# Retention followed by a Mish feed-forward layer: the opening rearranged (warm-up, copy of q, pools of the last y and the first h, state 4)

## The chip, the cores and the metric

The kernel runs on one core of one Trainium2 chip. The metric is device time in microseconds of one execution, the median of several runs. The engines are TensorE (PE in the profile; its weight loads are PEld), VectorE (DVE), ScalarE (ACT), GpSimd (POOL) and SyncE (SP), which here only issues transfers.

## The reference

Inputs are q, k and v of shape (4, 8, 768, 64) (batch, heads, tokens, head size) and two weight matrices. Per batch and head a 64x64 state is carried from token to token, and its output goes through a feed-forward layer:

```
gamma[h] = 1 - 2**(-5-h);  scale = 1/sqrt(64)
for t in range(768):
    state = gamma * state + outer(k[t], v[t])
    y[t]  = scale * q[t] @ state
x = y, heads side by side          # 3072 x 512
h = x @ w_in                       # 3072 x 2048
g = h * tanh(softplus(h))          # Mish
out = g @ w_out                    # 3072 x 512, float32
```

## The kernel before, in words

The tokens are taken in 24 chunks of 128. Within a chunk the recurrence is written with matmuls: scores of q and k, a triangular mask, "present" (masked scores times v), "past" (q times the state before the chunk), and the state's update ("outer" product of k and v, added to the old state, times gamma**128, the tile gcm). Powers of gamma are put into q and v when they are cast to fp16. Two heads share the 128 partitions, so a chunk has 4 pairs of heads (HP = 4).

Chunks are grouped in blocks: the first has 4 chunks (512 tokens), each of the ten others 2. For a block the finished y is copied from PSUM into an fp16 tile xt, from there `g1` makes h in units of 512 PSUM columns, `mish` on ScalarE turns each unit into g, and `g2_mm` with `g2_out` makes the output rows. From block 3 on the second product uses seven products in place of eight (`seven`); nothing there is changed. Attention work of the next block is put between the matmuls of the current one by hand-written plans (step number: functions). The order of all instructions on each engine is the order in the program (`manual_schedule`), and waits come from the tiles that they share.

Two PSUM pools matter: `mmps` (tag mm, 4 buffers of one bank) and `atps` (tag at, 2 buffers of two banks).

The first block (`first_block`, L642) is the opening, and it is built differently. Its q comes in two transfers of four heads each, with four successive tokens on each partition (`load_first_q`, L181). VectorE multiplies and casts it (L193), TensorE transposes it in 8 transposes for each half (L199), and `first_q_out` (L202) copies the result from PSUM into qfirst_t, putting the tokens back in their natural order as it writes. Half 0 of that copy is on ScalarE (L207), half 1 on VectorE (L209). k and v come with two successive tokens on a partition. ScalarE casts k (`cast_two`, L224) and copies its transposes (`turned_two`, L243); GpSimd casts v (L227). `scores_half` (L248) makes the scores of half the heads for two chunks, and `mask_half` (L261) masks them on VectorE with tri_first. `outer_first`, `state_first` (here the old state is added by an identity matmul on TensorE, L283, and VectorE multiplies by gcm, L285), `present_first` and `past_first` make y for two chunks in one tile y_ps of the at pool. `xt_out` (L304) copies y into xt: chunks 0 and 1 in one ScalarE copy, chunk 2 on ScalarE, chunk 3 on VectorE. The first two units of h are made half by half (`first_g1`, L635), in two tiles of the mm pool.

TensorE is kept busy before and between these steps by matmuls whose results are thrown away: `spin` (L339, fp16 with the identity) and `spin_wide` (L346, fp32 with the triangular mask tri). The constants ident, tri and tri_first are built by GpSimd in this order (L84 to L97). The weights w_in are loaded in slices, and each slice is cast to fp16 in halves: the first half by GpSimd, all others by VectorE (`cast_win`, L158).

Chunk 4, the first of block 1, is worked on near the end of block 0: `outer_state` (L424) makes its outer product and calls `state` (L387), where VectorE adds the old state (L394) and multiplies by gcm (L395).

Of the kernel before, what the change touches and what calls it, by code (L numbers as in the profile page):

```python
# [16 lines left out]
def kernel(  # L17
# [9 lines left out]
    nc = tc.nc  # L27
# [9 lines left out]
    R = 2  # L37
    HB = P // R
    BLOCKS = [4] + [2] * ((NCK - 4) // 2)
    first = [sum(BLOCKS[:i]) for i in range(len(BLOCKS))]  # L40
# [41 lines left out]
    gcm = cpool.tile([P, HP, P], FP32, name="gcm")  # L82
    warm = cpool.tile([P, 1], FP32, name="warm")
    nc.gpsimd.memset(ident, 0.0)  # L84
    nc.gpsimd.affine_select(
# [6 lines left out]

    tri_first = cpool.tile([P, R, C], FP32, name="tri_first")
    nc.gpsimd.memset(tri_first, 0.0)
    for c in range(2):
        t = tri_first[c * HB:(c + 1) * HB]
        nc.gpsimd.affine_select(  # L97
            out=t, in_=t, compare_op=ALU.is_gt, fill=1.0, base=0,
            pattern=[[1, R], [-1, C]], channel_multiplier=R)
    nc.vector.memset(warm, 0.0)  # L100
# [8 lines left out]

    qfirst_t = cpool.tile([P, HP, TB], FP16, name="qfirst_t")  # L110
    raw, k16s, v16s, t16s, kts, amf = {}, {}, {}, {}, {}, {}
# [89 lines left out]

    def first_q_out(half, t_ps, eng):  # L202
        n = HP // 2
        dst = qfirst_t[:, half * n:(half + 1) * n].rearrange("p i (t r) -> p i t r", r=CPB)
        src = t_ps.rearrange("p i r t -> p i t r")
        if eng is nc.scalar:
            nc.scalar.copy(dst, src)  # L207
        else:
            eng.tensor_copy(dst, src)  # L209

# [37 lines left out]
    def scores_half(s, half, at):  # L248
        for j in range(HP // 2):
            i = half * (HP // 2) + j  # L250
            for r in range(R):
                for c in range(2):
                    g = 2 * s + c
                    for hh in range(2):
                        o = slice(64 * hh, 64 * hh + 64)
                        nc.tensor.matmul(
                            at[toks(c), hh, j, r], kts[s][o, i, r, toks(c)],
                            qfirst_t[o, i, g * C:(g + 1) * C], start=True, stop=True,
                            skip_group_check=True)

    def mask_half(s, half, at):  # L261
        am = amf[s, half] = tpp.tile([P, 2, HP // 2, R, C], FP16, name="am")
        nc.vector.tensor_tensor(  # L263
            am.rearrange("p a j r t -> p (a j) (r t)"),
            at.rearrange("p a j r t -> p (a j) (r t)"),
            tri_first.rearrange("p r t -> p (r t)").unsqueeze(1).broadcast_to(
                (P, HP, R * C)), op=ALU.mult)
# [19 lines left out]
    def present_first(s, y, pairs):  # L287
        for i in pairs:
            half, j = divmod(i, HP // 2)
            for r in range(R):  # L290
                for c in range(2):
                    for hh in range(2):
                        nc.tensor.matmul(
                            y[64 * hh:64 * hh + 64, c, i], v16s[s, half][toks(c), r, 2 * j + hh],
                            amf[s, half][toks(c), hh, j, r], start=i == 0 and r == 0,
                            stop=s == 0 and c == 0 and r == R - 1, skip_group_check=True)

    def past_first(g, y):
        for i in range(HP):
            nc.tensor.matmul(  # L300
                y[:, g % 2, i], states[g - 1][:, i], qfirst_t[:, i, g * C:(g + 1) * C],
                start=False, stop=True, skip_group_check=True)

    def xt_out(g, y, eng, n=1):  # L304
        if eng is nc.scalar:
            nc.scalar.copy(xts[0][:, g:g + n], y[:, g % 2:g % 2 + n])
        else:
            eng.tensor_copy(xts[0][:, g:g + n], y[:, g % 2:g % 2 + n])

# [29 lines left out]
    def spin(at, n):  # L339
        for i in range(0, n, HP):  # L340
# [3 lines left out]
                ident.unsqueeze(1).broadcast_to((P, m, P)), start=True, stop=True)  # L344

    def spin_wide(at, n):  # L346
        nc.tensor.matmul(  # L347
            at[:, 0].rearrange("p j r t -> p (j r) t")[:, :n], tri,
            tri.unsqueeze(1).broadcast_to((P, n, C)), start=True, stop=True)

# [73 lines left out]
    def outer_state(g):  # L424
        outer(g, atps.tile([P, 2, HP, P], FP32, name="u_ps", tag="at")[:, 0])
        state(g)

# [19 lines left out]
    def y_two(blk):  # L447
# [6 lines left out]
        for j in range(2):  # L454
            present(a + j, lambda i: y_ps[:, i, j], lambda i: False)
        xts[blk] = xtp.tile([P, HP, TB], FP16, name="xt")
        nc.scalar.copy(  # L457
            xts[blk][:, :, :2 * C], y_ps.rearrange("p i j c -> p i (j c)"))

# [5 lines left out]
    def g1(blk, u):  # L465
# [3 lines left out]
        for j in range(per):  # L469
            s, f = divmod(u * per + j, FPS)  # L470
            for bp in range(NBP):
                nc.tensor.matmul(  # L472
                    h_ps[:, j], win(s, f, bp), xt(blk, bp),
                    start=(bp == 0), stop=(bp == NBP - 1))
        mish(blk, u, h_ps)

    def xt(blk, bp):
        return xts[0][:, :, bp] if blk == 0 else xts[blk][:, bp, :BLOCKS[blk] * C]

# [18 lines left out]
    def g2_out(o_ps, blk, t, due, cols=slice(None)):  # L498
        osb = op.tile(list(o_ps.shape), FP32, name="osb", tag="osb")
        nc.vector.tensor_copy(osb, o_ps)  # L500
        row0 = (first[blk] + t) * P
        dst = out[row0:row0 + P, cols]
        stores.append((due, dst, osb))
# [130 lines left out]

    def first_g1(h_ps, u, s):  # L635
        t = slice(s * TB // 2, (s + 1) * TB // 2)
        for bp in range(NBP):
            nc.tensor.matmul(  # L638
                h_ps[:, 0, t], win(0, u, bp), xts[0][:, 2 * s:2 * s + 2, bp],
                start=bp == 0, stop=bp == NBP - 1, skip_group_check=True)  # L640

    def first_block():  # L642
# [6 lines left out]
        load_weights()  # L649
        xts[0] = xtp.tile([P, CPB, HP, C], FP16, name="xt")  # L650

        at = at_tile()
        spin_wide(at, HP)
        spin_wide(at, HP)
        spin(at, 8)
        tq = turn_first_q(qf, 0)
        spin_wide(at, 3)
        first_q_out(0, tq, nc.scalar)
        tq = [tq, turn_first_q(qf, 1)]
        cast_two("k", 0, 0)  # L660
        turn_two(0, 0)
        first_q_out(1, tq[1], nc.vector)
        turned_two(0, 0)
        cast_two("k", 0, 1)
        spin_wide(at, 3)
        scores_half(0, 0, at)
# [5 lines left out]
        at = at_tile()  # L672
        spin_wide(at, 3)
        scores_half(0, 1, at)
# [9 lines left out]
        mask_half(1, 0, at)  # L684
        y = atps.tile([P, 2, HP, C], FP32, name="y_ps", tag="at")
        present_first(0, y, range(HP))
        turn_two(1, 1)
        turned_two(1, 1)
        state_first(1)
        past_first(1, y)  # L690
        xt_out(0, y, nc.scalar, 2)
        for half in range(2):
# [4 lines left out]
        mask_half(1, 1, at)  # L697
        y = atps.tile([P, 2, HP, C], FP32, name="y_ps", tag="at")
        outer_first(1)
        state_first(2)  # L700
        present_first(1, y, range(HP // 2))
        h_ps = [mmps.tile([P, 1, TB], FP32, name="h_ps", tag="mm") for _ in range(2)]
        first_g1(h_ps[0], 0, 0)
        present_first(1, y, range(HP // 2, HP))
# [3 lines left out]
        xt_out(3, y, nc.vector)  # L708
        first_g1(h_ps[1], 1, 0)
        cast_win(0, 1, nc.vector)  # L710
        for u in range(2):
            first_g1(h_ps[u], u, 1)
            mish(0, u, h_ps[u])
        state_first(3)
# [114 lines left out]
```

## Time and profile before

| | |
|---|---|
| median of 3 runs | 207.05 us (206.41 to 207.69) |
| the profiled execution's own time | 207.59 us |
| its span, first to last instruction | 205.80 us |
| busy share of the span | PE 96%, PEld 73%, DVE 58%, ACT 43%, POOL 39% |
| chain that ended last | PE 89%, DVE 5%, ACT 3% |
| mean granted TensorE clock | 0.999 |
| DMA | 38.60 MB, mean 188 GB/s |

Times within the profile are counted from the start of the span. The chain is followed back from the last instruction: at each step to what released it, or to the instruction before it on its engine. "issue" is time in which an engine waited for nothing that the profile shows. The busy time of a matmul reaches to its modelled end, and the next one starts before it; so the spacing of two starts tells what a matmul adds to a row of them, and its duration (0.2 us more or less longer) tells when its result is there. Transfers are told by issue and landing; the landings are in the trace.

### The profile page before, as it was taken

The numbers are of one execution on the slowest core, as the hardware profiler recorded it, in microseconds if no ns is written. First come the engines' busy times: TensorE is split into PE (matmuls) and PEld (weight loads), VectorE is DVE, ScalarE is ACT, GpSimd is POOL, SyncE is SP. The second block draws the span as 40 slices with busy tenths as digits, with TensorE's granted clock in tenths as the row PEclk, the third lists the DMA queues.
The fourth block names the chain that finished last, engine by engine and source line by source line (L and its number), as shares of the span: only waits on it lengthen the run. The fifth ranks groups of instructions, "written<-read, shape, count | busy, mean of one in ns | idle before, by whom it ended". The sixth has DMA issues, their size and how long they took to land.

```text
span 205.8 us, 4678 instructions
## 1 busy us (share of the span) xinstructions
PE 198.3 (96%) x1975; PEld 150.9 (73%) x1975; DVE 120.4 (58%) x179; ACT 87.7 (43%) x147; POOL 79.5 (39%) x74
## 2 busy tenths in 40 slices
PE   6988999999999999999999999999999999999993
PEld 2556444456855865888888888888888888898882
DVE  3686644168027987775686773575684773573062
ACT  2462763242621631453453453453453453552640
POOL 4261000519954757647477066077077000000000
PEclk9999999999999999999999999999999999999999
DMA  5999999998999999999795892996794800200202
GB/s 183 298 317 361 387 387 276 293 214 177 208 258 259 210 197 242 221 211 227 168 253 92 201 256 56 205 206 105 188 242 83 204 3 3 102 2 27 78 25 76
DMA packets 95892, 38.60 MB, mean 188 GB/s; under 512 B 82304, under 2 KB 89984, under 8 KB 95872
## 3 DMA queue, kind: packets, MB, share of 16 engines
q1 hardware_dynamic: 92608, 37.50, 77.8%
q10 hardware_dynamic: 3264, 0.82, 2.3%
q8 instruction: 15, 0.25, 0.5%
q14 instruction: 5, 0.04, 0.1%
HBM read 27.30 MB, written 6.29 MB: 163 GB/s over the span
## 4 chain that ended last, share of the span: by engine, by line
PE 89%; DVE 5%; ACT 3%; issue 1%; POOL 0%; POOLq 0%
PE h_ps L472 40%; PE o_ps L571 22%; PE o_ps L494 11%; PE at L368 3%; PE y_ps L411 2%; PE at L347 2%; PE y_ps L401 2%; PE u_ps L382 2%; DVE am L374 1%; DVE gsum L541 1%; ACT xt L457 1%; PE h_ps L638 1%; ACT g L488 1%; DVE am L263 1%; ACT qk L224 1%
## 5 line engine op out<-in xcount | busy, mean ns | idle before, releaser
L472 PE MATMUL h_ps<-xt,win 128*128 128x256 f16 (+1 forms) x696 | 86.1, 281 | 0.3
L488 ACT ACTIVATE g<-h_ps 128x512 f16<-128x512 f32 x96 | 57.2, 597 | 57.4 <-PE h_ps L472 56.0
L472 PEld LDWEIGHTS <-win 128*128 128x128 f16 x696 | 67.3, 98 | 15.4 <-issue 0.8
L316 POOL TENSOR_TENSOR qk<-qf,qvs 128x512 f16<-128x512 f32 x20 | 21.7, 1086 | 61.0 <-DMA qf<-in_q_dram 55.7
L374 DVE TENSOR_TENSOR am<-at,tri 128x1024 f16<-128x1024 f32 x20 | 23.6, 1219 | 15.8 <-PE at L368 15.6
L494 PE MATMUL o_ps<-wout,g 128*128 128x512 f16 x128 | 30.1, 380 | 0.0
L321 POOL TENSOR_SCALAR qk<-kf 128x512 f16<-128x512 f32 x18 | 28.6, 1587 | 3.7 <-DMA kf<-in_k_dram 2.7
L571 PEld LDWEIGHTS <-gsum 128*128 128x128 f16 x256 | 24.2, 98 | 4.4 <-DVE gsum L541 1.0
L322 POOL TENSOR_TENSOR v<-vf,qvs 128x512 f16<-128x512 f32 x20 | 21.9, 1094 | 6.3 <-DMA vf<-in_v_dram 4.9
L571 PE MATMUL o_ps<-tmat,gsum 128*128 128x256 f16 x192 | 23.9, 273 | 0.3
L494 PEld LDWEIGHTS <-g 128*128 128x128 f16 x128 | 11.7, 98 | 13.0 <-issue 0.3
L585 DVE TENSOR_TENSOR osb<-o_ps,snap 128x256 f32<-128x256 f32 x24 | 10.1, 421 | 18.3 <-ACT snap L577 15.1
L571 PEld LDWEIGHTS <-g 128*128 128x128 f16 x192 | 18.8, 98 | 2.2
L457 ACT CAST xt<-y_ps 128x1024 f16<-128x1024 f32 x10 | 10.1, 1012 | 22.8 <-PE y_ps L411 15.5
L540 DVE TENSOR_TENSOR gsum<-g 128x512 f16<-128x512 f16 x16 | 7.3, 454 | 14.2 <-ACT g L488 14.2
L571 PE MATMUL o_ps<-wout,g 128*128 128x256 f16 x128 | 15.3, 273 | 0.0
L577 ACT COPY snap<-o_ps 128x256 f32<-128x256 f32 x24 | 8.9, 372 | 14.4 <-PE o_ps L571 13.0
L394 DVE TENSOR_TENSOR su<-u_ps,st 128x512 f32<-128x512 f32 x13 | 9.0, 691 | 4.5 <-PE u_ps L382 4.3
L395 DVE TENSOR_TENSOR st<-su,gcm 128x512 f16<-128x512 f32 x13 | 10.8, 832 | 0.4
L541 DVE TENSOR_TENSOR gsum<-gsum,g 128x512 f16<-128x512 f16 x16 | 8.8, 551 | 0.5
L347 PE MATMUL at<-tri 128*128 128x384 f32 (+1 forms) x10 | 6.6, 767 | 1.9 <-POOL tri L89 1.9
L571 PE MATMUL o_ps<-tmat,g 128*128 128x256 f16 x64 | 8.3, 272 | 0.0
(72 smaller groups left out, 150.2 us busy)
## 6 DMA issues: line engine op xcount, KB each, us to landing
kf<-in_k_dram SPq DMA_DIRECT2D x23, 256.0 KB, 4.7
vf<-in_v_dram SPq DMA_DIRECT2D x23, 256.0 KB, 4.9
out_dram<-osb SPq DMA_DIRECT2D x22, 256.0 KB, 3.4
qf<-in_q_dram SPq DMA_DIRECT2D x19, 256.0 KB, 4.0
wt<-in_moe_w_out_dram SPq DMA_DIRECT2D x3, 1024.0 KB, 8.9
wi<-in_moe_w_in_dram SPq DMA_DIRECT2D x4, 512.0 KB, 7.6
wi<-in_moe_w_in_dram SPq DMA_DIRECT2D x2, 1024.0 KB, 11.9
qfirst<-in_q_dram SPq DMA_DIRECT2D x2, 512.0 KB, 4.6
```

Source lines behind the costliest of these rows:

```text
L316: nc.gpsimd.tensor_tensor(q16, qf, qs.unsqueeze(2).broadcast_to((P, H, D)), op=ALU.mult)
L321: nc.gpsimd.tensor_scalar(k16, kf, BOOST, None, op0=ALU.mult)
L322: nc.gpsimd.tensor_tensor(v16, vf, vs.unsqueeze(2).broadcast_to((P, H, D)), op=ALU.mult)
L347: nc.tensor.matmul(at[:, 0].rearrange("p j r t -> p (j r) t")[:, :n], tri, tri.unsqueeze(1).broadcast_to((P, n, C)), start=True, stop=True)
L374: nc.vector.tensor_tensor(am, ats.pop(g), tri.unsqueeze(1).unsqueeze(1).broadcast_to((P, 2, HP, C)), op=ALU.mult)
L395: nc.vector.tensor_tensor(st, su, gcm, op=ALU.mult)
L457: nc.scalar.copy(xts[blk][:, :, :2 * C], y_ps.rearrange("p i j c -> p i (j c)"))
L472: nc.tensor.matmul(h_ps[:, j], win(s, f, bp), xt(blk, bp), start=(bp == 0), stop=(bp == NBP - 1))
L488: nc.scalar.activation(gt, h_ps, AF.Mish, scale=inv_boost3)
L494: nc.tensor.matmul(o_ps, gts[blk, fb][:, t * P:(t + 1) * P], wouts[s][:, f, cols], start=(fb == 0), stop=(fb == NFB - 1))
L541: nc.vector.tensor_tensor(s2, s1, a11, op=ALU.subtract)
L571: nc.tensor.matmul(o_ps, x(f), w(f), start=first and f == 0, stop=f == n - 1, skip_group_check=True)
```

## The change

- **Constants.** GpSimd builds tri_first first, then ident, then tri. tri_first has a new order of its columns.
- **Warm-up.** `spin_wide` is gone. `spin(at, 36)` issues nine 128x512 fp16 matmuls with ident before the first q transposes, and `spin(at, 4)` one more at three later places, twelve in all.
- **q.** `first_q_out` copies without reordering, both halves on VectorE. qfirst_t keeps the tokens in the order of the transposes: token 4t+r stands at column (r, t). Scores and past read 4 pieces of 32 columns; y comes out in that order too.
- **xt of block 0** becomes one row of 512 columns for each pair of heads, in the order (r, t). `xt_out` writes 32 columns at a time; chunks 0 and 1 are two ScalarE copies instead of one. The first block's output rows are stored with a stride of four rows.
- **Pools.** y of chunks 2 and 3 is two tiles of the mm pool, and the first two units of h are one tile of the at pool (they were the other way round). Unit 0 of h is made in two halves, unit 1 in one piece after it; the half of unit 1 that was made before the last y was copied is gone.
- **State 4.** `outer_state` adds the old state with an identity matmul on TensorE, as the opening does; VectorE only multiplies by gcm.

```diff
+    Q0 = C // CPB
+    tri_first = cpool.tile([P, R, CPB, Q0], FP32, name="tri_first")
+    nc.gpsimd.memset(tri_first, 0.0)
+    for c in range(2):
+        t = tri_first[c * HB:(c + 1) * HB]
+        nc.gpsimd.affine_select(
+            out=t, in_=t, compare_op=ALU.is_gt, fill=1.0, base=0,
+            pattern=[[1, R], [-1, CPB], [-CPB, Q0]], channel_multiplier=R)
     nc.gpsimd.memset(ident, 0.0)
...
-    tri_first = cpool.tile([P, R, C], FP32, name="tri_first")
-    nc.gpsimd.memset(tri_first, 0.0)
...
-    qfirst_t = cpool.tile([P, HP, TB], FP16, name="qfirst_t")
+    qfirst_t = cpool.tile([P, HP, CPB, P], FP16, name="qfirst_t")
...
-    def first_q_out(half, t_ps, eng):
-        n = HP // 2
-        dst = qfirst_t[:, half * n:(half + 1) * n].rearrange("p i (t r) -> p i t r", r=CPB)
-        src = t_ps.rearrange("p i r t -> p i t r")
-        if eng is nc.scalar:
-            nc.scalar.copy(dst, src)
-        else:
-            eng.tensor_copy(dst, src)
+    def first_q_out(half, t_ps):
+        nc.vector.tensor_copy(qfirst_t[:, half * (HP // 2):(half + 1) * (HP // 2)], t_ps)
...
-                            qfirst_t[o, i, g * C:(g + 1) * C], start=True, stop=True,
+                            qfirst_t[o, i, :, g * Q0:(g + 1) * Q0], start=True, stop=True,
...
-                y[:, g % 2, i], states[g - 1][:, i], qfirst_t[:, i, g * C:(g + 1) * C],
+                y[g % 2][:, i], states[g - 1][:, i], qfirst_t[:, i, :, g * Q0:(g + 1) * Q0],
...
-    def xt_out(g, y, eng, n=1):
+    def xt_out(g, y, eng):
+        dst = xts[0].rearrange("p i (r c t) -> p c (i r) t", r=CPB, c=CPB)[:, g]
+        src = y[g % 2].rearrange("p i (r t) -> p (i r) t", r=CPB)
         if eng is nc.scalar:
-            nc.scalar.copy(xts[0][:, g:g + n], y[:, g % 2:g % 2 + n])
+            nc.scalar.copy(dst, src)
         else:
-            eng.tensor_copy(xts[0][:, g:g + n], y[:, g % 2:g % 2 + n])
+            eng.tensor_copy(dst, src)
...
     def outer_state(g):
-        outer(g, atps.tile([P, 2, HP, P], FP32, name="u_ps", tag="at")[:, 0])
-        state(g)
+        u = us[g] = atps.tile([P, 2, HP, P], FP32, name="u_ps", tag="at")[:, 0]
+        _, k16, v16, _ = cast[g]
+        for i in range(HP):
+            nc.tensor.matmul(
+                u[:, i], k16[:, 2 * i:2 * i + 2], v16[:, 2 * i:2 * i + 2],
+                start=i == 0, stop=False, skip_group_check=True)
+        nc.tensor.matmul(u, ident, states[g - 1], start=False, stop=True, skip_group_check=True)
+        states[g] = stp.tile([P, HP, P], FP16, name="st")
+        nc.vector.tensor_tensor(states[g], us.pop(g), gcm, op=ALU.mult)
...
-        dst = out[row0:row0 + P, cols]
+        if blk == 0:
+            dst = out[:TB].rearrange("(p r) c -> r p c", r=CPB)[t]
+        else:
+            row0 = (first[blk] + t) * P
+            dst = out[row0:row0 + P, cols]
...
-    def first_g1(h_ps, u, s):
-        t = slice(s * TB // 2, (s + 1) * TB // 2)
+    def first_g1(h_ps, u, s=None):
+        t = slice(0, P) if s is None else slice(s * HB, (s + 1) * HB)
         for bp in range(NBP):
             nc.tensor.matmul(
-                h_ps[:, 0, t], win(0, u, bp), xts[0][:, 2 * s:2 * s + 2, bp],
+                h_ps[:, u].rearrange("p (r t) -> p r t", r=CPB)[:, :, t], win(0, u, bp),
+                xts[0][:, bp].rearrange("p (r t) -> p r t", r=CPB)[:, :, t],
                 start=bp == 0, stop=bp == NBP - 1, skip_group_check=True)
...
-        xts[0] = xtp.tile([P, CPB, HP, C], FP16, name="xt")
+        xts[0] = xtp.tile([P, HP, TB], FP16, name="xt")
         at = at_tile()
-        spin_wide(at, HP)
-        spin_wide(at, HP)
-        spin(at, 8)
+        spin(at, 36)
         tq = turn_first_q(qf, 0)
-        spin_wide(at, 3)
-        first_q_out(0, tq, nc.scalar)
+        spin(at, 4)
         tq = [tq, turn_first_q(qf, 1)]
         cast_two("k", 0, 0)
         turn_two(0, 0)
-        first_q_out(1, tq[1], nc.vector)
+        first_q_out(0, tq[0])
+        first_q_out(1, tq[1])
         turned_two(0, 0)
         cast_two("k", 0, 1)
-        spin_wide(at, 3)
+        spin(at, 4)
         scores_half(0, 0, at)
...
-        spin_wide(at, 3)
+        spin(at, 4)
         scores_half(0, 1, at)
...
         y = atps.tile([P, 2, HP, C], FP32, name="y_ps", tag="at")
+        y = [y[:, c] for c in range(2)]
         present_first(0, y, range(HP))
...
-        xt_out(0, y, nc.scalar, 2)
+        for c in range(2):
+            xt_out(c, y, nc.scalar)
...
-        y = atps.tile([P, 2, HP, C], FP32, name="y_ps", tag="at")
         outer_first(1)
         state_first(2)
+        y = [mmps.tile([P, HP, C], FP32, name="y_ps", tag="mm") for _ in range(2)]
         present_first(1, y, range(HP // 2))
-        h_ps = [mmps.tile([P, 1, TB], FP32, name="h_ps", tag="mm") for _ in range(2)]
-        first_g1(h_ps[0], 0, 0)
+        h_ps = atps.tile([P, 2, TB], FP32, name="h_ps", tag="at")
+        first_g1(h_ps, 0, 0)
         present_first(1, y, range(HP // 2, HP))
         past_first(2, y)
         past_first(3, y)
         xt_out(2, y, nc.scalar)
         xt_out(3, y, nc.vector)
-        first_g1(h_ps[1], 1, 0)
         cast_win(0, 1, nc.vector)
-        for u in range(2):
-            first_g1(h_ps[u], u, 1)
-            mish(0, u, h_ps[u])
+        first_g1(h_ps, 0, 1)
+        mish(0, 0, h_ps[:, :1])
+        first_g1(h_ps, 1)
+        mish(0, 1, h_ps[:, 1:])
         state_first(3)
```

More of the change, by code (lines that the diff above doesn't have):

```diff
@@ L91 @@
         pattern=[[-1, C]], channel_multiplier=1)
-    tri_first = cpool.tile([P, R, C], FP32, name="tri_first")
-    nc.gpsimd.memset(tri_first, 0.0)
[L95 to L99, printed above, removed]
     nc.vector.memset(warm, 0.0)
@@ L265, in mask_half @@
             at.rearrange("p a j r t -> p (a j) (r t)"),
-            tri_first.rearrange("p r t -> p (r t)").unsqueeze(1).broadcast_to(
+            tri_first.rearrange("p r a t -> p (r a t)").unsqueeze(1).broadcast_to(
                 (P, HP, R * C)), op=ALU.mult)
@@ L293, in present_first @@
                         nc.tensor.matmul(
-                            y[64 * hh:64 * hh + 64, c, i], v16s[s, half][toks(c), r, 2 * j + hh],
+                            y[c][64 * hh:64 * hh + 64, i], v16s[s, half][toks(c), r, 2 * j + hh],
                             amf[s, half][toks(c), hh, j, r], start=i == 0 and r == 0,
@@ L344, in spin @@
                 ident.unsqueeze(1).broadcast_to((P, m, P)), start=True, stop=True)
[L346 to L349, printed above, removed]
     def turn(g):
@@ L455, in y_two @@
             present(a + j, lambda i: y_ps[:, i, j], lambda i: False)
-        xts[blk] = xtp.tile([P, HP, TB], FP16, name="xt")
+        xt = xtp.tile([P, HP, TB], FP16, name="xt")
+        xts[blk] = xt
         nc.scalar.copy(
-            xts[blk][:, :, :2 * C], y_ps.rearrange("p i j c -> p i (j c)"))
+            xt[:, :, :2 * C], y_ps.rearrange("p i j c -> p i (j c)"))
     def win(s, f, bp):
@@ L472, in g1 @@
                 nc.tensor.matmul(
-                    h_ps[:, j], win(s, f, bp), xt(blk, bp),
+                    h_ps[:, j], win(s, f, bp), xts[blk][:, bp, :nt],
                     start=(bp == 0), stop=(bp == NBP - 1))
         mish(blk, u, h_ps)
-    def xt(blk, bp):
-        return xts[0][:, :, bp] if blk == 0 else xts[blk][:, bp, :BLOCKS[blk] * C]
     def mish(blk, u, h_ps):
@@ L500, in g2_out @@
         nc.vector.tensor_copy(osb, o_ps)
-        row0 = (first[blk] + t) * P
-        dst = out[row0:row0 + P, cols]
+        if blk == 0:
[3 more added lines that the diff above has]
+            dst = out[row0:row0 + P, cols]
         stores.append((due, dst, osb))
```

## The prediction

> **What bounds the kernel now.** I read the page first: TensorE is busy 96% of the span, VectorE 58%, ScalarE 43%, and the chain that ended last is 89% TensorE. The end of the kernel is therefore set by TensorE's own order, except where it waits. Nearly all edits lie in the first 21 us, so I then read the chain in order of time, and after it the timeline of that stretch. The chain of waits, columns start us, length us, what:
>
> ```profile
> 1.85 3.78 PE at L347 x4
> 5.63 0.85 PE at L342 x2
> 6.48 0.87 PE t_ps L199 x8
> ...
> 7.37 1.01 ACT qfirst_t L207
> 8.38 0.54 ACT qk L224
> ...
> 8.97 0.41 PE t_ps L238 x4
> ...
> 9.40 0.58 ACT qkt L243
> 9.99 0.54 ACT qk L224
> ...
> 18.32 0.96 issue
> 19.28 1.36 PE h_ps L638 x11
> 20.64 0.22 PE u_ps L283
> 20.86 12.09 PE h_ps L472 x56
> ```
>
> Up to 20.5 us the path hops between engines: warm-up, q transposes, ScalarE's copy of q, ScalarE's cast of k, TensorE, ScalarE's copy of k, scores. From 20.86 us TensorE runs on without a hole to 49 us, so what the opening saves arrives there whole if the weights keep up. The timeline of the same stretch (start, length, engine, line, operation, in brackets the idle time before it) has the pieces that change:
>
> ```profile
> 7.37 1.01 ACT L207 COPY qfirst_t<-t_ps 128x1024 f16<-128x1024 f16 x1 [4.75 <-PE t_ps L199]
> 8.66 1.23 DVE L209 COPY qfirst_t<-t_ps 128x1024 f16<-128x1024 f16 x1 [1.12 <-PE t_ps L199]
> 10.04 0.42 PE L256 MATMUL at<-qfirst_t,qkt 64*64 64x128 f16 x16
> 18.25 0.58 ACT L306 CAST xt<-y_ps 128x512 f16<-128x512 f32 x1 [2.26 <-PE y_ps L300]
> 18.86 0.69 DVE L308 CAST xt<-y_ps 128x512 f16<-128x512 f32 x1 [1.45 <-ACT xt L306]
> 40.54 0.69 DVE L359 COPY qkt<-t_ps 128x1024 f16<-128x1024 f16 x1 [4.75 <-PE t_ps L357]
> 45.09 0.69 DVE L394 TENSOR_TENSOR su<-u_ps,st 128x512 f32<-128x512 f32 x1 [0.39 <-PE u_ps L382]
> ```
>
> The reader is to see three things: the reordering copies of q cost 1.01 and 1.23 us where a plain copy of the same size costs 0.69 (L359); the two casts of the last y stand one behind the other; and TensorE stops 0.96 us at 18.32 with no named releaser. For that stop, the queue table:
>
> ```profile
> q8 instruction: 15, 0.25, 0.5%
> ```
>
> Fifteen packets for 3950 weight loads and matmuls is one per 263. The trace has the first at 16.65 us, taking 1.13; TensorE stops after its 447th instruction and resumes at 19.28. I read the stop as TensorE waiting for its own program.
>
> **The change part by part.**
>
> **Warm-up start.** GpSimd now builds the score mask first: a memset of 0.30 and two selects, 0.85 together. Then comes the identity, 0.20 and 0.29, with gaps of about 0.07. Ident is ready at about 2.55 instead of tri at 1.79, so TensorE starts near 2.6. Nine 128x512 fp16 matmuls at L342's spacing of 0.427 (5.422 to 5.849) take 3.84 and end at 6.45; before, the wide fp32 ones and two fp16 ones ended at 6.28. The first transposes move 0.2 later; VectorE had their data at 6.10. If the clock is granted where it was (the trace's record starts at 7.49), the one spin that follows takes about 0.29 instead of the 0.88 of the fp32 pair at L347 (7.13 to 8.01), so the second eight transposes start at 7.63, not 8.01, and end at 8.24. If the grant is tied to the start of the work, it comes at 8.24 and they end near 8.75: I keep both.
>
> **q copy.** Both halves go to VectorE at 0.69 (L359). The first waits for the second q multiply (ends 7.54): 7.59 to 8.28, the second to 8.97. ScalarE loses its 1.01. Its k cast needs only the load, which landed at 7.19, and so is done by 7.9; the k transposes follow the q ones, end at 8.5, ScalarE's k copy ends at 9.12, and the scores start near 9.17 instead of 10.04: 0.87 earlier. This does not all survive. The third k load landed at 10.81, so that cast starts at 10.86, not 11.49: 0.63 is left. From here the chain is the old one (cast, transposes, copy, scores, masks and states on VectorE), shifted by 0.64. The POOL v casts end 11.25 and 14.76, before their users at 12.1 and 15.1. The win cast on POOL is held by its load (15.05 to 16.09), so the first h matmuls start at 16.19 instead of 16.70. That costs 0.13 of the shift, leaving 0.51: the past matmuls end at 17.70 instead of 18.21. Matmuls that read q as 4x32 columns I price like contiguous ones; the nearest row is L472, which already reads xt in 4 pieces at 0.216 each. The upper bound is a doubling of 64 scores and 12 past matmuls, about 0.5 us on the path.
>
> **Swapped pools.** The last two y's get a bank each, so ScalarE's cast waits for chunk 2 only and VectorE's runs 17.74 to 18.43 instead of 18.86 to 19.55. What TensorE then has to do is more: four h matmuls of 256 columns at 0.108 and four of 512 at 0.216, 1.30 us, where eight of 256 (0.87) were left, because unit 1's first half used to run inside the wait. From data alone the stage ends at 18.48 + 1.30 = 19.78, against 20.48. The program, however: the order of instructions puts the 447th within the same four matmuls, after the first. The packet that must land is asked for, I take it, one period of about 250 instructions earlier, in the scores at 13.39; those move by 0.63, so TensorE resumes at 18.65 instead of 19.28. Then 3 x 0.108 + 0.864 gives 19.84: 0.64 earlier. Two casts of 0.58 in place of one of 1.02 on ScalarE have until 16.19 and end at 15.5. The VectorE win cast for unit 2 ends at 19.03, needed at 20.05. The next one needs VectorE's state 3 first, done as before about 0.6 after the h matmuls, then 0.68; its load landed at 19.43. Later loads land at 20.93, 23.62 and 26.31 and are needed from 23.5, 25.2 and 28.7: covered. If they came later, each would stop TensorE for its whole lateness. SP's first w_out load is freed about 1.1 earlier but queues behind win loads that land until 26.31, so nothing.
>
> **State 4.** One more identity matmul of 128x512 on TensorE: 0.216 (L472 spacing; L283 is the same instruction). VectorE drops one add, 0.69, and reads PSUM instead of su. Before, the mask behind it ended at 48.21 and its reader came at 48.71, so the VectorE saving is not on the path. Cost 0.22, inside the unbroken TensorE stretch.
>
> **At nothing.** The first output's row order changes addresses, not sizes, and stores wait for nobody there; the mask has the same shape; matmuls reading contiguous xt were already at 0.216.
>
> **Sum.** -0.64 + 0.22 = -0.42. The profiled execution took 207.59 (span 205.80 and 1.79 around it): 207.17. It lies 0.54 above the median of the runs, 207.05, so against the median: 206.6. About 1% is what a measurement of this kernel can tell from no change.
>
> The Trainium skill (Runtime: NRT & Kernel Launch, Instruction fetch mechanics) says that blocks of 256 instructions are fetched while the current one runs and that the crossing is mostly hidden; the 0.96 stop speaks against "hidden" here. By the rule alone the resume would be free and the result 0.06 lower.
>
> **The rivals.**
>
> *The program packet does not move.* If its arrival is set by the loaded DMA queues and not by when it is asked for, TensorE still resumes at 19.28, ends the stage at 20.47, and 0.22 is lost for state 4: 207.3. For: DMA is full there (share 1.09 to 1.15 of 16 engines), and the packet ran 3.3 us after the 13.39 that I take for its request. Against: the second packet also came 3.9 us after its own.
>
> *The clock is granted a stage later: slower.* Before, TensorE worked from 1.85 and got the full clock at 7.49, after 5.6 us of work with one block of eight transposes in it. Now it starts at 2.6, and from 6.45 mostly transposes and short spins follow. If the grant is missed, transposes and matmuls stay at the cold spacing (0.107 and 0.427 instead of 0.056 and 0.216) until the dense stretch has lasted as long. TensorE pieces on the chain from 8.97 to 20.86 sum to 6.0 us, about half of it spacing: +3.0. After 20 us, 5.6 us at half speed lose up to 2.8. With 1 to 2 of that: 206.6 + 4.5 = about 211. It decides if the grant falls after about 9.5. Against: the spins still give 3.9 us unbroken before the transposes, and a grant tied to the start (8.24) leaves only 0.25 of the gain unclaimed. The Trainium skill (TensorE: Matmul & The Clock Gate, Parts 1 and 4) has a free-running window of 3.4 us and says that transposes do not count as busy. By that rule the new opening would miss some phases of the window; the one record here, at 7.49, fits both readings.
>
> *Nothing arrives.* The opening ends earlier but a load holds a weight cast: 207.0 to 207.3, as above, most likely at the third win slice, with about 0.2 to spare.
>
> **How the numbers follow.** Forecast (shift arrives, 205.9 to 207.0): 0.62. Packet or load holds it (207.0 to 207.6): 0.22. Clock later: 0.08. The rest: a larger gain, if unnamed gaps close too, 0.08, of which 0.03 beyond 1%. The three runs of before spread 0.6 either way, so the range is 205.8 to 207.9. Faster by over 1% 0.03, within 1% 0.88, slower 0.09.
>
> **What would show it.** Right: first TensorE work at 2.6; two VectorE copies of 0.69; scores at 9.2, third k cast at 10.9; VectorE's xt cast beside ScalarE's; the L472 stretch beginning near 20.2 instead of 20.86; one more 0.22 near 45. Wrong: cold spacing after 9.5; the stop still ending at 19.3; a stop before u 4 or u 8 of the first h stage on a win cast; q-reading matmuls spaced over 0.056.

## The result, and the profile after

The changed kernel took 208.23 us (median of 6 runs, 207.89 to 208.44) against 207.18 for the kernel before beside it (6 runs, 206.41 to 207.69). The ratio is 1.0049, with an interval of 1.0026 to 1.0072: slower by about half a per cent, and above the range that was forecast. The profiled execution took 208.18, with a span of 206.4 us; that of before took 207.59.

The chain of waits of the changed kernel (start, length, what), for the stretch in which the gain was forecast:

```profile
8.95 5.98 DMA wi<-in_moe_w_in_dram
...
14.99 1.05 POOL win L162
...
16.08 0.61 PE h_ps L638 x4
16.69 0.35 PE y_ps L288 x16
17.04 0.57 PE y_ps L295 x8
...
17.63 0.70 DVE xt L305
...
18.38 0.63 PE h_ps L638 x4
...
19.02 0.61 ACT g L485
...
19.67 1.02 PE h_ps L638 x4
20.70 0.22 PE u_ps L278
20.91 12.09 PE h_ps L472 x56
...
45.11 0.22 PE u_ps L423
```

Three things are new. The chain no longer comes through the warm-up and the copies of q: until 16.08 it is a load, the first win slice, and GpSimd's cast of it. In the first product there is now a step on ScalarE: the Mish of unit 0 (L485) stands between unit 0's matmuls and unit 1's. And the added identity matmul of state 4 (L423) is there with its 0.22. The long stretch begins at 20.91 instead of 20.86; the forecast had it near 20.2.

The timeline of the changed kernel shows the pieces that were forecast:

```profile
7.40 1.49 DVE L204 COPY qfirst_t<-t_ps 128x1024 f16<-128x1024 f16 x2
...
9.06 0.42 PE L251 MATMUL at<-qfirst_t,qkt 64*64 64x128 f16 x16 [0.46 <-ACT qkt L238]
...
17.41 0.58 ACT L303 CAST xt<-y_ps 128x512 f16<-128x512 f32 x1 [2.10 <-PE y_ps L295]
17.63 0.69 DVE L305 CAST xt<-y_ps 128x512 f16<-128x512 f32 x1 [0.95 <-PE y_ps L295]
...
18.38 0.61 PE L638 MATMUL h_ps<-xt,win 128*128 128x256 f16 x4 [0.79 <-DVE xt L305]
...
19.02 0.60 ACT L485 ACTIVATE g<-h_ps 128x512 f16<-128x512 f32 x1 [1.03 <-PE h_ps L638]
19.67 1.02 PE L638 MATMUL h_ps<-xt,win 128*128 128x512 f16 x4 [0.69 <-ACT g L485]
```

The two copies of q take 1.49 together, the scores start at 9.06, and the two casts of xt run side by side. The bracket of the last line is what the forecast lacked: TensorE sat idle for 0.69 us until ScalarE's Mish of unit 0 was done. No stop of TensorE for its own program is left in this stretch. Its packet began at 15.97 instead of 16.65.

### The profile page after: what moved, and what is told of

Read it like the earlier page. It is cut to its first block, busy times and chain, and to the rows that moved or that the text cites. A ratio compares the mean times of both kernels' runs of the same rounds, so it can differ in the third digit from the quotient of the medians.

```text
span 206.4 us, 4676 instructions
## 1 busy us (share of the span) xinstructions
PE 196.4 (95%) x1972; PEld 149.1 (72%) x1972; DVE 119.2 (58%) x179; ACT 87.1 (42%) x147; POOL 79.7 (39%) x74
## 4 chain that ended last, share of the span: by engine, by line
PE 83%; DVE 5%; SPq 4%; DMA 3%; ACT 2%; issue 1%; POOL 1%; ACTq 0%
PE h_ps L472 40%; PE o_ps L571 21%; PE o_ps L491 11%; SPq L208 3%; DMA wi<-in_moe_w_in_dram 3%; PE at L360 3%; PE y_ps L403 2%; PE y_ps L393 2%; DVE gsum L541 2%; PE u_ps L374 1%; ACT g L485 1%; PE h_ps L638 1%; ACT xt L457 1%; DVE gsum L540 1%; DVE am L366 1%
## 5 line engine op out<-in xcount | busy, mean ns | idle before, releaser
L485 ACT ACTIVATE g<-h_ps 128x512 f16<-128x512 f32 x96 | 57.3, 597 | 58.2 <-PE h_ps L472 56.1
L313 POOL TENSOR_TENSOR qk<-qf,qvs 128x512 f16<-128x512 f32 x20 | 22.4, 1122 | 61.9 <-DMA qf<-in_q_dram 53.5
L318 POOL TENSOR_SCALAR qk<-kf 128x512 f16<-128x512 f32 x18 | 27.9, 1551 | 3.0 <-DMA kf<-in_k_dram 1.8
L457 ACT CAST xt<-y_ps 128x1024 f16<-128x1024 f32 x10 | 10.1, 1012 | 23.1 <-PE y_ps L403 15.7
L386 DVE TENSOR_TENSOR su<-u_ps,st 128x512 f32<-128x512 f32 x12 | 8.3, 691 | 4.1 <-PE u_ps L374 3.9
L541 DVE TENSOR_TENSOR gsum<-gsum,g 128x512 f16<-128x512 f16 x16 | 9.5, 597 | 0.5
L387 DVE TENSOR_TENSOR st<-su,gcm 128x512 f16<-128x512 f32 x12 | 8.9, 739 | 0.4
L571 PE MATMUL o_ps<-wout,gsum 128*128 128x256 f16 x64 | 8.3, 273 | 0.0
```

Source lines behind the costliest of these rows:

```text
L313: nc.gpsimd.tensor_tensor(q16, qf, qs.unsqueeze(2).broadcast_to((P, H, D)), op=ALU.mult)
L318: nc.gpsimd.tensor_scalar(k16, kf, BOOST, None, op0=ALU.mult)
L457: nc.scalar.copy(xt[:, :, :2 * C], y_ps.rearrange("p i j c -> p i (j c)"))
L485: nc.scalar.activation(gt, h_ps, AF.Mish, scale=inv_boost3)
L541: nc.vector.tensor_tensor(s2, s1, a11, op=ALU.subtract)
L571: nc.tensor.matmul(o_ps, x(f), w(f), start=first and f == 0, stop=f == n - 1, skip_group_check=True)
```

## The experiments

Two quantities are read in every trace: when the first matmul of the first product starts ("first h"), and how long it takes from there to the identity matmul of state 3, after which TensorE runs on without a hole.

**The wait on the Mish, state 4, and before once more.** Theory: the 0.69 us come from the one tile that both units of h share, and state 4 adds 0.22. Rivals: the opening of before, as profiled, was late and is usually better; or another wait takes the place of each.

e1_mish_behind, the changed kernel with the Mish moved:

```diff
-        mish(0, 0, h_ps[:, :1])
         first_g1(h_ps, 1)
+        mish(0, 0, h_ps[:, :1])
         mish(0, 1, h_ps[:, 1:])
```

> The changed kernel with one edit: the Mish of unit 0 of h is issued behind the matmuls of unit 1, so that these no longer wait for it. Theory A (TensorE's stop of 0.69 us before the four 512-column matmuls, 18.99 to 19.67, is the prediction's missed wait and is worth its whole length): the matmul of state 3 begins near 19.85 instead of 20.53, time 0.6 to 0.7 below the changed kernel, about 207.5, which is 0.3 above the kernel before. Theory B (the loads of the weights are next behind it): TensorE stops later on a cast of w_in instead, and the time stays within 0.2 of 208.2.

e2_state4_vector, the changed kernel with state 4 as before; e3_both has the edits of e1 and e2:

```diff
     def outer_state(g):
-        u = us[g] = atps.tile([P, 2, HP, P], FP32, name="u_ps", tag="at")[:, 0]
...
-        nc.vector.tensor_tensor(states[g], us.pop(g), gcm, op=ALU.mult)
+        outer(g, atps.tile([P, 2, HP, P], FP32, name="u_ps", tag="at")[:, 0])
+        state(g)
```

> The changed kernel with state 4 added on VectorE again, as before the change. Theory A (the identity matmul costs its 0.216 us on TensorE and the add on VectorE is hidden): 0.2 below the changed kernel, about 208.0. Rival: VectorE's add and multiply, slowed beside GpSimd as in the trace of before (1.26 us for the multiply), now reach the masks: same as the changed kernel or slower.

> The changed kernel with both edits: Mish of unit 0 behind unit 1's matmuls, and state 4 on VectorE. If the two costs add: 0.9 below the changed kernel, about 207.3 by the median of its runs, and the dense stretch begins 0.64 earlier than before the change. If what the changed kernel lost lies mainly elsewhere, in VectorE's sums running beside GpSimd around 92 us (a step of 0.30 in the trace), it stays 0.3 to 0.5 above that.

b0_before_again is the kernel before, unchanged:

> The kernel before, unchanged, for a second profile of it and for the width of a comparison with itself. Theory C (its opening depends on when the full clock is granted, 7.49 us in the first profile, and so its runs spread over 1.3 us, while the opening of the changed kernel is held by the load of the first weights and spreads over 0.5): a clock granted earlier goes with a stage end before 20.48 and a span below 205.8, by up to 0.5. Theory D (the spread comes from VectorE's sums beside GpSimd near 90 to 107 and 152): stage end at 20.48 whatever the clock, and a different number of VectorE sums that take over 0.7 us instead of 0.42.

| | median us | ratio to before | first h | to state 3 |
|---|---|---|---|---|
| changed kernel (first result) | 208.23 | 1.0049 [1.0026, 1.0072] | 16.08 | 4.45 |
| e1_mish_behind | 207.71 | 1.0020 [1.0006, 1.0033] | 16.09 | 3.61 |
| e2_state4_vector | 208.18 | 1.0050 [1.0032, 1.0068] | 16.18 | 4.53 |
| e3_both | 207.48 | 1.0011 [0.9996, 1.0027] | 16.11 | 3.61 |
| b0_before_again | 207.16 | 1.0005 [0.9991, 1.0019] | 16.15 | 3.83 |
| before (the page of the prediction) | | | 16.70 | 3.78 |

The chain of e1 goes from VectorE's cast straight on; unit 1's matmuls follow unit 0's:

```profile
17.64 0.70 DVE xt L305
...
18.39 1.47 PE h_ps L638 x8
19.86 0.22 PE u_ps L278
```

With the Mish moved the stretch takes 3.61 instead of 4.45: 0.84 less. In the whole time e3 wins 0.70 over e2, and e1 wins 0.52 over the changed kernel, so this loss is real. The price of state 4 is seen in the traces alone: behind its matmul e2 has gained 0.22 on the changed kernel. e3's median is 0.23 under e1's, but their runs overlap too much to tell that from nothing. e2 won nothing in the end: against the changed kernel its trace lost 0.71 at 73.7 us, by a late transpose (below), and won 0.62 back in two later places, near 93 and 154 us.

b0 brought the second surprise. Its chain is that of before, but not its times:

```profile
0.72 4.07 DMA qfirst<-in_q_dram
...
6.17 0.63 PE t_ps L199 x8
6.82 1.01 ACT qfirst_t L207
...
16.22 0.54 PE h_ps L638 x4
...
17.66 0.11 PE h_ps L638
17.77 1.01 issue
18.78 1.36 PE h_ps L638 x11
```

The same instructions come 0.5 earlier than on the page that the prediction argued from. There the q transposes ran at the slow clock and took 0.87 from 6.48; here they take 0.63 from 6.17. In the trace's record of the granted clock, full speed came at 5.25 here and at 7.49 there. So the kernel before reaches its first h at 16.15 in a good execution, where the changed kernel, held by a load, starts it at 16.08. The cut-off kernel t1 (below) is of the late kind again, with 16.71.

**Cut off behind block 1.** To read the opening without what follows, blocks 2 to 10 are left out of the next four:

```diff
-    for blk in range(1, len(BLOCKS)):
+    for blk in range(1, 2):
...
-        plan = plan_of(blk)
+        plan = {}
```

t1 is before, t2 the changed kernel, t3 and t4 have the edits of e1 and e3.

> The kernel before, cut off behind block 1: blocks 2 to 10 are left out (their loads, attention, products and output rows), and block 1 prepares no next block. It ends near 66 us and shows the opening, block 0 and state 4 without the chance events of the later blocks. Reference for the three that follow. If its opening follows the clock (Theory C), its runs spread by about 0.5 us or more.

> The changed kernel, cut off in the same way. Theory A and C together (TensorE's wait for Mish 0.69 to 0.8, state 4 0.22, and an opening of before that is usually 0.3 to 0.5 faster than in its first profile): 0.6 to 0.9 above the cut-off kernel before, and a narrow spread. Rival (most of the 1.0 between the two medians comes from the later blocks, where loads and VectorE's sums happen to collide): 0.1 to 0.4 above.

> The changed kernel with Mish of unit 0 behind unit 1's matmuls, cut off in the same way. Theory A: 0.7 to 0.85 below the cut-off changed kernel, which makes it level with the cut-off kernel before or up to 0.2 below. In the full kernel the same edit brought 0.5 by the medians; if it brings its whole length here, the later blocks take the difference back.

> As the one before it, with state 4 added on VectorE again. If TensorE's identity matmul costs its 0.216 in full: 0.2 below the one before, and 0.2 to 0.4 below the cut-off kernel before. In the full changed kernel the same edit brought nothing that could be told (208.18 against 208.23).

Medians: 69.67 (69.17 to 69.82), 70.18, 70.23 and 70.39. The expectation for t3 and t4 failed, although TensorE's last matmul came earlier: 64.24 in t2, 63.32 in t3, 63.17 in t4. The chain of t3 says why:

```profile
58.63 5.17 DMA out_dram<-osb
63.91 0.69 DVE osb L497
```

The last copy waits for a free osb buffer, hence for a store. That store took 5.17 and 5.35 to land in t3 and t4; in t1 and t2 it took 4.03 and 4.00, and there the chain ends with TensorE. So the times of the short kernels do not price the opening; their traces do. First h to state 3 took 3.78, 4.45, 3.61 and 3.61, as in the whole kernels. t2 and t3 had their clock at 8.0, and their scores came at 9.4, not 9.1, but first h at 16.17 and 16.10: the load hides that.

**Later stores.** e3 is 0.26 earlier than b0 at state 3 but ends later. Its chain shows where it is lost:

```profile
64.61 1.02 ACT xt L450
...
66.33 0.73 SPq L129
...
67.17 6.42 DMA qkt<-qk
...
73.64 0.40 PE at L360 x8
```

TensorE waits for the scores' transposed q and k, whose transfer SP issued at 67.17; in before it was 65.44. That costs e3 0.69 against b0; of two later steps one gives back 0.30, the other costs 0.36. Four stores stand ahead of the transfer in SP's queue, as they do in before. In e3 SP's loads between them also waited for ScalarE's copy of xt, the first line above. s3 (on e3) and s0 (on before) put the stores off:

```diff
-                    g2_out(o_tiles[t], 0, t, 1)
+                    g2_out(o_tiles[t], 0, t, 9)
```

> The whole kernel with the Mish of unit 0 behind the matmuls of unit 1 and state 4 back on VectorE, and block 0's stores due at step 9 of block 1 instead of step 1. In e3_both 0.64 to 0.70 us were lost at 73.6 us, where TensorE waits for the fourth DMA transpose, which SP issued at 67.17 (65.44 in the profile of before). Theory 1 (the four stores that SP issues at 58.6 to 61.2 push the transposes and the loads behind them back): the fourth transpose is issued before 66, the step at 73.6 falls under 0.2 us, median 206.7 to 207.0 against 207.48 of e3_both, so faster than before by 0.2 to 0.5. Theory 2 (the order of SP's loads and GpSimd's casts alone decides it, or the stores come back later in the way of others): step of 0.5 or more at 73 to 75 us or at a later place, median 207.3 to 207.7.

> The kernel before, whole, with block 0's stores due at step 9 of block 1 instead of step 1, and nothing else changed. Theory 1 (TensorE waits little for the fourth transpose in before, since its opening ends later): 207.0 to 207.3, the same as before. Theory 2 (the stores hold before back as well): 206.6 to 206.9. Theory 3 (the later stores collide with the next ones): over 207.5.

210.9 us, ratio 1.0143 [1.0116, 1.017], and 209.9, ratio 1.0101 [1.0079, 1.0124]. The transfer was issued at 63.82 and 63.84, as theory 1 wanted. But s3's time is far above both of its theories, and s0's is theory 3's: VectorE then waited for a free osb buffer, with its masks queued behind that copy. The chain of s3:

```profile
68.35 4.82 DMA out_dram<-osb
73.25 0.69 DVE osb L490
```

**The parts, cut off.** p1 is before with the constants' order and the fp16 warm-up alone; p3 is the changed kernel with its pools put back. Both leave out blocks 2 to 10.

```diff
-        y = [mmps.tile([P, HP, C], FP32, name="y_ps", tag="mm") for _ in range(2)]
+        y = atps.tile([P, 2, HP, C], FP32, name="y_ps", tag="at")
+        y = [y[:, c] for c in range(2)]
...
-        h_ps = atps.tile([P, 2, TB], FP32, name="h_ps", tag="at")
+        h_ps = [mmps.tile([P, 1, TB], FP32, name="h_ps", tag="mm") for _ in range(2)]
```

> The kernel before, cut off behind block 1 (blocks 2 to 10 left out), with only the change's first part: the constants in its order and the 12 plus 8 plus 9 warm-up matmuls in fp16, q still copied by ScalarE with its turn, the pools and state 4 as before. Theory 1 (the opening of before runs at the pace of ScalarE's q copies and of TensorE's clock, and the warm-up alone brings nothing): first scores at 9.5 to 10.1, state 3 at 20.0 to 20.5, like t1_before_short (10.05 and 20.485) or up to 0.5 earlier where the clock is granted before 7; median 69.2 to 69.8. Theory 2 (the warm-up makes the clock late): clock granted after 7.9, scores after 10.1, median 69.9 or more. Theory 3 (the warm-up's matmuls themselves bring the gain of the opening): scores by 9.2.

> The changed kernel, cut off behind block 1 (blocks 2 to 10 left out), with its pools put back as before: the last y of state 3's side from the at pool, the first product's units 0 and 1 in a tile of their own each from the mm pool, and unit 1's first four matmuls ahead of VectorE's copy of xt. Theory 1 (the wait on ScalarE's Mish comes from the tile that the two units share in the swapped pools): no wait of TensorE for the Mish, state 3 at 19.5 to 19.8 against 20.625 of t2_after_short, TensorE's last matmul 0.8 to 1.1 us earlier (63.1 to 63.4 against 64.24), though the time may be held at 69.4 to 70.3 by the last stores, as in t3_after_mish_short. Theory 2 (a stop of TensorE's program, not the shared tile, ends at about 20.5): state 3 at 20.3 or later, last matmul at 64.0 or later.

Medians 70.05 and 70.04. These two, s3, s0 and the next four ran on another chip than the runs above (the second chip, below), where the first win load lands about 0.5 later and before took 207.65 and 207.9; t1 and p1 can't be set against each other. p1's clock came at 8.55, its scores at 10.58 and its first h at 17.23, late in all three. That is one execution. Its clock came 5.91 after its first work; in t1, with the old warm-up, it came 5.91 after the first work too, so the late clock is no sign against the new one. In p3 the stretch took 3.78, as in before: no wait for the Mish, but VectorE's cast of xt again 0.62 behind ScalarE's. My 19.5 to 19.8 for state 3 (it was 20.47) had overlooked that, besides the later load.

**With more buffers, and one part undone in the whole kernel.** s4 and s5 are s3 and s0 with `bufs=9` instead of 5 in the pool of osb. f1 is the whole changed kernel with its pools put back, w1 is e3 with the old warm-up.

> The whole kernel with the Mish of unit 0 behind the matmuls of unit 1, state 4 back on VectorE, block 0's stores due at step 9 of block 1 instead of step 1, and 9 osb buffers instead of 5, so that no copy of VectorE waits for a store. Theory 1 (SP issues the stores of block 0 ahead of the third and fourth transposes and their loads, and that costs e3_both its 0.64 to 0.70 us at 73.6): the fourth transpose is issued at 63.5 to 64.5, as in s3_both_later_stores, TensorE loses under 0.2 us between 66 and 80, and the ratio to before is 0.995 to 0.998. Theory 2 (the loads' rate and GpSimd's casts set the transposes, whatever the stores do): a step of 0.5 or more between 66 and 80, ratio 1.000 or more. Theory 3 (the stores, later, collide with the next stage): step under 0.2 at 73.6 but one of 0.4 or more after 80, ratio 1.000 or more.

> The kernel before, whole, with block 0's stores due at step 9 of block 1 and 9 osb buffers, nothing else changed. Theory 1: the fourth transpose is issued near 64 instead of 65.4 to 66.2, which before does not need: ratio 0.998 to 1.001. Theory 2: ratio 1.000 to 1.003, with the steps of before. Theory 3: over 1.003 with a new step after 80.

> The whole changed kernel with only its pools put back: the last y in one tile of the at pool, units 0 and 1 of the first product in a tile of their own each, unit 1's first four matmuls ahead of VectorE's copy of xt. If the swap only made the wait on the Mish, state 3 comes 0.8 earlier than in the changed kernel and the ratio to before is 1.000 to 1.002. If the swap also took away VectorE's wait of 0.62 us for ScalarE's copy of xt out of the shared y tile, as the cut-off kernel p3 showed, the one makes up for the other within 0.2 us: state 3 at 20.3 to 20.6 and the ratio 1.003 to 1.006, near the changed kernel's.

> The whole kernel with the Mish of unit 0 behind the matmuls of unit 1, state 4 back on VectorE, and the warm-up of before (the constants' order, the wide fp32 matmuls) with the change's VectorE copies of q. If the warm-up is worth nothing beside the loads: scores at 9.0 to 9.2, state 3 at 19.6 to 19.8, ratio to before 0.999 to 1.003, as e3_both. If the later, shorter warm-up is what lets the transposes of q begin early: scores at 9.5 to 10, state 3 at 20 or later where the third k load does not hide it, ratio 1.002 to 1.005.

| | median us | ratio to before | first h | to state 3 |
|---|---|---|---|---|
| s4_both_stores_buffers | 207.86 | 0.9989 [0.9969, 1.0008] | 16.60 | 3.61 |
| s5_before_stores_buffers | 208.00 | 0.9998 [0.9979, 1.0018] | 16.65 | 3.83 |
| f1_after_pools_back | 208.14 | 1.0000 [0.9979, 1.0021] | 16.60 | 3.78 |
| w1_both_old_warm_up | 207.85 | 1.0008 [0.9982, 1.0034] | 16.63 | 3.61 |

In s4 the fourth transpose is issued at 63.78 and the stop at 73 us is gone: with the stores out of its way and buffers to spare, TensorE runs on from the first product into the scores.

```profile
66.17 7.15 PE h_ps L465 x64
73.31 0.55 PE at L360 x16
73.87 2.70 PE o_ps L484 x12
```

Yet hardly any gain is left in the time, and in the trace 0.48 is lost 20 us on (against b0). The timeline of s4:

```profile
90.64 1.04 POOL L313 TENSOR_TENSOR qk<-qf,qvs 128x512 f16<-128x512 f32 x1 [2.05 <-DMA qf<-in_q_dram]
90.98 0.98 DVE L533 TENSOR_TENSOR gsum<-g 128x512 f16<-128x512 f16 x1 [0.86 <-ACT g L478]
...
92.00 0.71 DVE L534 TENSOR_TENSOR gsum<-gsum,g 128x512 f16<-128x512 f16 x1
...
92.77 0.39 PE L564 MATMUL o_ps<-tmat,gsum 128*128 128x256 f16 x2 [0.27 <-DVE gsum L534]
```

Two VectorE sums took 0.98 and 0.71 in s4 where each takes 0.42 with GpSimd idle. In b0 the second sum began just ahead of GpSimd's operation, and took no longer:

```profile
91.17 0.42 DVE L541 TENSOR_TENSOR gsum<-gsum,g 128x512 f16<-128x512 f16 x1
91.24 1.25 POOL L316 TENSOR_TENSOR qk<-qf,qvs 128x512 f16<-128x512 f32 x1 [2.04 <-DMA qf<-in_q_dram]
```

By its steps theory 3 held: none at 73 us, one of 0.48 at 92. By its ratio neither theory did: 0.9989 lies between theory 1's (0.998 at most) and theory 3's (1.000 or more). But the step at 92 is not the price of the cure: s5, the kernel before with the same stores and buffers, has it too (0.49 against b0). Set against s5, s4 is 0.28 earlier at state 3 and 0.29 earlier at TensorE's last matmul. In this pair of traces the opening's gain is kept, though the medians, 207.86 and 208.00, do not tell it from nothing.

s5 itself came out as its theory 1 had it. f1's state 3 came at 20.38, as the second branch of its expectation had it, and its ratio of 1.0000 as the first; with w1 the scores came at 9.62, as with the new warm-up on this chip (9.58 in f1), so the old warm-up costs nothing there. (The ratios on record are not exactly the quotients of the medians.) Seven of the eight traces on this chip, all but p1's, have first h at 16.60 to 16.69, those with before's opening (s0 and s5, 16.65) among them. With the changed opening the win load ends last there; in s0 and s5 GpSimd's cast of that load ends at 16.60, only 0.05 before TensorE comes to it.

**The swap of the pools, side by side** on a further chip, in whole kernels: the changed kernel again, and f1's once more.

> The changed kernel unchanged, once more, side by side with the one that has only its pools put back (the next run), to price the swap of the pools on one chip. From the first product's first matmul to state 3's it took 4.45 us with the swap and 3.78 without. If these 0.67 us arrive whole: ratio to before 1.004 to 1.006, and 0.5 to 0.8 us over the next run. If the later waits (transposes near 74 us, VectorE's sums) level the two: under 0.3 us apart.

> The changed kernel with only its pools put back, as f1_after_pools_back, beside the changed kernel on the same chip. If the swap is what makes the change slow: ratio to before 1.000 to 1.003 and 0.5 to 0.8 us under the changed kernel. If not: ratio 1.004 or more.

208.33 us, ratio 1.0059 [1.0043, 1.0075], and 207.67, ratio 1.0027 [1.0013, 1.0041]. So the swap costs 0.66 on one chip, and the stretch differs by 0.67 (4.45 and 3.78). That the two numbers agree so well is luck. Between the two profiles f2 loses 0.47 of its lead at 74 us, by the late transpose (issued at 67.01, against 65.60), and gets 0.30 back near 93 and 0.23 near 139. The timeline of f2 shows the other side of the swap:

```profile
17.81 0.58 ACT L303 CAST xt<-y_ps 128x512 f16<-128x512 f32 x1 [2.32 <-PE y_ps L295]
18.43 0.69 DVE L305 CAST xt<-y_ps 128x512 f16<-128x512 f32 x1 [1.57 <-ACT xt L303]
18.78 1.42 PE L638 MATMUL h_ps<-xt,win 128*128 128x256 f16 x11 [0.90 <-issue]
```

In the old pools VectorE's cast waits for ScalarE's, as both read one y tile. TensorE has unit 1's first half to do meanwhile, and its program stop lies there too. The swap trades that wait for one on the Mish, and takes the work away that had filled it.

## Why the prediction was wrong, step by step

**Warm-up and q copy: right in their times.** First work at 2.72 (forecast 2.6), scores at 9.06 (9.17), third k cast at 10.76 (10.86), first h at 16.08 (16.19), VectorE's xt cast at 17.63 (17.74). Against the page that the forecast started from, first h came 0.62 earlier, more than the 0.51 that was forecast. But the page was one execution, and a late one. Against b0 this part is worth 0.07, and on the second chip about as little (16.60 for 16.65). Of the traces with before's opening on a chip whose first win load landed near 15, two had 16.70 (before and t1) and one 16.15, so what the part is worth in the median of many runs is not known. I had one of the first kind, and its late clock stood in its own record. One reading beside it was off, without effect: ScalarE's 1.01 for its half of q is not the price of the reordering, since its copy of xt, with as many elements, takes 1.01 as well (L457).

**Swapped pools: the step that failed.** "From data alone the stage ends at 18.48 + 1.30 = 19.78" counted matmuls and left out a wait. Units 0 and 1 of h are now one tile. ScalarE reads the first half of it for the Mish while TensorE is to write the second, and waits come from the tile. So TensorE waited for the whole Mish, a wait that the forecast put at nothing without a reason. The 0.69 idle in front of the four 512-column matmuls put state 3 at 20.53: 0.05 later than on the page of before, where 0.64 earlier (19.84) was forecast. e1 removes that wait alone, and state 3 comes at 19.70, as forecast or a little before. f1, f2 and p3, with a tile for each unit, do not have it either. The page of before showed the same thing in the y tile, VectorE's cast waiting for ScalarE's ("<-ACT xt L306"). I read that as a cost that the swap removes, and did not ask which two engines meet in the new shared tile.

The Trainium skill (PSUM — Partial Sum Buffer, Specifications and PSUM bank collisions raise a hardware error) has PSUM guarded by bank and quadrant, with a bank of 2 KiB in each partition. By its size, 512 fp32 numbers, each unit fills a bank of its own, so by that rule the two halves need no guard against each other. The trace has a wait all the same: the tile made it.

**The program packet: it moved,** by 0.69 from the page for a forecast of 0.63, but by only 0.15 from b0, and where the order was put back the stop ended at 18.78 (f2; 18.65 forecast), as it does in b0. In all nine traces with the old order of the matmuls TensorE stops behind its 447th instruction and resumes 2.56 to 2.70 after the packet's start, which itself lies anywhere from 16.11 to 17.17. That speaks for the reading that TensorE waits for its program, and against the rival of a packet that does not move; no run was made to prove it. In the changed kernel no stop shows, since TensorE stands in the other waits.

**State 4: right.** 0.217 in the trace against b0. The medians do not resolve it (e1 and e3, above).

**The sum.** Against b0's trace: opening -0.07, the stretch from first h to state 3 +0.62 (4.45 for 3.83), state 4 +0.22, and +0.36 near 92 us. Together +1.13; the spans differ by 1.07 (206.37 and 205.30) and the medians by 1.05. The last term was not in the prediction. Against the page's own trace the terms are +0.05 at state 3, +0.22 and +0.30, together 0.57 for a forecast of -0.42. In the changed kernel a sum of VectorE meets a cast of GpSimd there:

```profile
91.81 1.04 POOL L313 TENSOR_TENSOR qk<-qf,qvs 128x512 f16<-128x512 f32 x1 [3.24 <-DMA qf<-in_q_dram]
91.98 1.15 DVE L541 TENSOR_TENSOR gsum<-gsum,g 128x512 f16<-128x512 f16 x1
...
93.19 0.33 PEld L571 LDWEIGHTS <-gsum 128*128 128x128 f16 x4 [0.43 <-DVE gsum L541]
```

**The rivals.** "Nothing arrives" named the third win slice as the load that holds the path. The load that did was the first, which the forecast itself had counted (16.19), and it does not explain why the kernel became slower. The late clock did not happen in the changed kernel (6.87, where the forecast had kept 7.49 and 8.24). At 8.0, in t2 and t3, it cost 0.3 at the scores and nothing at first h.

**What stays open:** how much the later first work (2.72 for 1.85) delays the clock in the mean of many executions, and which of the late waits an execution meets. Among the ten traces with block 0's stores at their old step, SP issued the fourth transpose at 67.0 to 67.8 in e2, e3, f1, f2 and w1, and at 65.1 to 66.2 in before, b0, the changed kernel, a1 and e1; no run shows why. A kernel with y and both units of h in separate tiles was not tried, and none of those run is measurably faster than before.

## What to carry to other kernels

When a change makes two work items share a tile, ask for every reader and writer of that tile which engine now waits for which: the wait comes with the tile, even where the halves don't overlap. Look at a second profile of the kernel before, or at least at the moment of its clock grant, before a gain is measured from one opening. And when time won early seems lost at a later stop, compare with a kernel that has every other edit but not the early gain. In e3 the gain was lost at 73.6, to a transfer that came later. In s4 it seemed lost at 92, but s5 had the same stop, and against s5 the 0.28 was still there at the end.

## What the runs showed of the hardware

- **Clock grant.** Over 20 traces full speed came between 5.09 and 8.55 us. Counted from the first work it came after 3.24 to 5.91 with the old warm-up (6 traces) and after 2.82 to 5.91 with the new one (14). In every trace the stretch at full speed lasted a whole multiple of 3.413 us: 58 or 59 times in the whole kernels, 17 or 18 in the cut ones. Such a grid, with a start that differs between executions, lets the grant of one and the same kernel move by 3.4. The Trainium skill (TensorE: Matmul & The Clock Gate, Part 1) has a free-running window of 3.4 us; the traces agree with it, and one trace therefore can't tell a warm-up from its phase.
- **VectorE beside GpSimd.** In the changed kernel 32 sums of two 128x512 fp16 SBUF tiles were traced. The 16 that met no GpSimd operation took 0.42 or 0.43. Of the 16 that met one, eight took as little and eight 0.51 to 1.15. Each of the six that began inside a GpSimd multiply of two tiles ended 0.28 after it, whether they had begun 0.17 or 0.81 behind its start. The Trainium skill (SBUF — State Buffer, SBUF: two separate sides) has such a VectorE operation and a GpSimd operation share a port pair that only one holds at a time. The trace agrees in kind: the sum that took 1.15 at 91.98 began 0.17 after GpSimd's operation and ended 0.28 after it.
- **Loads differ by chip.** The first win slice landed at 14.93 in the changed kernel, 15.45 in s4 and 15.18 in a1, on other chips, and moved first h with it (16.08, 16.60 and 16.33).
